# Three K parts, then three V parts: one TensorE loop over all units, and ScalarE spreads the probabilities

## The chip, the cores and the metric

The kernel runs on one core of a Trainium2 chip. The metric is the device time of one execution in microseconds (us): the median of several runs. A profiled execution also gives a span, which is the time from the first to the last recorded instruction of the core, and a trace of what each engine and each DMA queue did in it.

## The reference, cut to what matters

Two independent blocks, A and B, each do one decode step of attention with cached keys and values. Both have 2 queries (the batch), 32 heads, 8192 cached tokens and a head size of 192, all in bfloat16:

```python
q = (x @ wq)                                  # x: (2, 1, 640), wq: (640, 32*192)
scores = einsum("bhqd,bhkd->bhqk", q, k_cache) * 192 ** -0.5
p = softmax(scores, axis=-1)
o = einsum("bhqk,bhkd->bhqd", p, v_cache)     # k_cache, v_cache: (2, 32, 8192, 192)
out = o.reshape(B, 1, 32 * 192) @ wo          # wo: (6144, 640)
# the outputs of A and B side by side: (2, 1, 1280)
```

Every cached key and value is used once, for one query. The kernel therefore reads some 837 MB for a small amount of arithmetic.

## The kernel before, in words

The work is cut into 16 units. A unit is one query and 8 heads of one block (4 units for a query, 4 queries over both blocks). The K cache of a unit is laid over 128 partitions, 16 partitions a head and 512 tokens a partition, and is cut into three parts (`c` = 0, 1, 2) of 64 KiB a partition, 8 MiB a part. The V cache of a unit is cut in the same way. There are three buffers of this size (`bufs`), so of the 96 K and V parts three are on the chip at a time.

The list `loads` sets the order in which SyncE issues the transfers, all on its own queue: the three K parts of unit 0, then V part 0 of unit u-1, K part 0 of unit u, V part 1 of unit u-1, K part 1 of unit u, and so on, at the end the three V parts of unit 15 and `wo` in pieces (`pieces`). Load i goes into buffer i modulo 3, and SyncE waits before issuing it until load i-3 has been used up (`done`): for a K part until TensorE has finished its sums (`("sl", u, c)`), for a V part until TensorE has finished its products (`("pv", u, c)`). So two loads are queued behind the one that is being used.

What is done with a K part: VectorE multiplies the cached keys in place by the query (`dve_mul`, line 303), in five pieces of 32 tokens a partition (`k` = 0 to 4, the last with 10 more tokens); where a token lies across two parts its fragments go into `pad` (line 301). TensorE sums 192 products to 16 with an identity as weights (`pe_sum`, line 420, three PSUM banks in turn; `pe_rest`, line 432, for the tokens left over, whose end is `("sl", u, c)`), and VectorE reduces the 16 to the score (`dve_red`, line 311), three pieces behind its multiplications. After the third part VectorE and GpSimd find the maximum (`dve_rest`, `dve_max`, `dve_mp`, `pool_ar`, `dve_nm`, `dve_nb`), ScalarE takes the exponentials (`act_exp`, line 366), and VectorE spreads them (`dve_spread`, line 338): it writes `pb`, in which each probability stands in one of 8 columns, its head's, and the other 7 are zero. TensorE forms the row sums (`pe_l`, line 438) and multiplies `pb` with the three V parts (`pe_pv`, lines 450 and 456). VectorE and ScalarE divide and store the result (`dve_rc`, `dve_ohi`, `dve_osum`, `act_of`), and TensorE places it among the results of the other units (`pe_pl`, line 462). TensorE also makes the query of the next unit (`pe_q`), which ScalarE copies to `qt` (`act_q`).

Each engine has a list of its own (`_Stream`), filled slot by slot with `put`, in the order in which the engine works; waits are on semaphores that every step raises. In slot u TensorE, VectorE and the others do unit u's K work and unit u-1's V work. `emit` writes slot 0 and slot 16 out and the slots between as one loop.

At the start the weights `wq` for A, the input `x`, `wq` for B and the first K part are transferred. The first projection needs an identity matrix, which GpSimd and VectorE make from a triangle of ones (`tri`). At the end `pe_out` multiplies by `wo`, and two transfers store the output.

Of the kernel before, what the change touches and what calls it, by code (L numbers as in the profile page):

```python
# [12 lines left out]
class _Stream:  # L13
    virtual = set()

    def __init__(self, name, sem, reg, first=3):
# [17 lines left out]
    def resolve(self):  # L34
        waited = {}
        out = []
        for fn, waits, has_sig, tag in self.ops:
            need = {}
            for key in waits:
                if key is None or (key in self.virtual and tag[0] < self.first):  # L40
                    continue
                sem, val = self.reg[key]
                sid = id(sem)
                if val <= waited.get(sid, 0):
                    continue
                if sid not in need or need[sid][1] < val:
                    need[sid] = (sem, val)
# [8 lines left out]
    def emit(self, eng, loops=()):  # L56
        ops = self.resolve()
# [12 lines left out]
        self._emit(eng, ops[pos:])  # L70

# [48 lines left out]
def build_kernel(nc, blocks, out):  # L120
# [30 lines left out]
    PO = 128 - UH  # L151
# [4 lines left out]
    with ExitStack() as es:  # L156
# [35 lines left out]
        tri = pb[0:HP, 2304:2304 + HP + 1]  # L192
# [21 lines left out]
        S_act = _Stream("act", sem("s_act"), reg, 1)  # L214
        S_dve = _Stream("dve", sem("s_dve"), reg, 1)
        S_pool = _Stream("pool", sem("s_pool"), reg, 1)
        bsem = [sem(f"bsem{i}") for i in range(NBUF)]
# [12 lines left out]
        for u in range(1, NU):  # L230
            for c in range(NCH):
                loads += [("v", u - 1, c), ("k", u, c)]
        loads += [("v", LASTU, c) for c in range(NCH)]
        buf = {}
        for i, key in enumerate(loads):
            buf[key] = i % NBUF
            reg[key] = (bsem[i % NBUF], 16 * (i // NBUF + 1))
        for kind, u, c in loads:
            if u:
                assert buf[kind, u, c] == buf[kind, 1, c] or (kind, u) == ("v", LASTU)  # L240
# [28 lines left out]
        def ld_kv(kind, u, c):  # L269
# [3 lines left out]
            return dma(bufs[buf[kind, u, c]], src[:, c * ROW:(c + 1) * ROW], (kind, u, c))  # L273
# [21 lines left out]
        def dve_mul(u, c, k):  # L295
            b = buf["k", u, c]

            def fn(eng):
                if k == 0:
# [30 lines left out]
        def dve_spread(ranges):  # L330
            dst = pb[:].rearrange("p (g a j h) -> p g a j h", a=2, j=4, h=UH)
            src = sc[:].rearrange("p (g j a) -> p g a j", j=4, a=2)

            def fn(eng):
                for lo, hi in ranges:
                    for a in range(2):
                        shape = [128, hi - lo, 4, UH]
                        ins = eng.tensor_tensor(dst[:, lo:hi, a], src[:, lo:hi, a].unsqueeze(3).broadcast_to(shape),  # L338
                                                mask[:].unsqueeze(1).unsqueeze(1).broadcast_to(shape), ALU.mult)
                return ins  # L340
            return fn
# [119 lines left out]
        def pe_pl(u):  # L461
            return lambda eng: eng.matmul(oacc_all[:, 0:Dh], place[:, S_pe.at(UH * u, 128, UH)], o_sb[:],
# [49 lines left out]
        S_pool.add(lambda eng: eng.memset(tri, 0.0), sig=("tri0",))  # L512
        S_pool.add(lambda eng: eng.memset(ident[:], 0.0))
        for n in range(1, HP + 1):
            S_pool.add((lambda n: (lambda eng: eng.memset(tri[0:n, n:n + 1], 1.0)))(n),
                       waits=[("tri0",)] if n == 1 else [], sig=("tri",) if n == HP else None)
# [3 lines left out]
        for n in range(128 // HP):  # L520
            S_dve.add((lambda r: (lambda eng: eng.tensor_tensor(ident[r, r], tri[:, 1:HP + 1], tri[:, 0:HP], ALU.subtract)))
                      (slice(HP * n, HP * n + HP)), waits=[("tri",)], sig=("id1",) if n == 128 // HP - 1 else None)
# [28 lines left out]
        S_act.add(act_q, waits=[("q", 0)], sig=("qe", 0))  # L551
# [17 lines left out]
        for u in range(NU + 1):  # L569
# [3 lines left out]
            def red(c, k):  # L573
                put("dve", u, ("r", c, k), dve_red(u, c, k), [("s", u, c, k), ("sp", u - 1) if u else None])

            def turn_out():
# [3 lines left out]
                put("act", u, ("of", -1), act_of, [("os", v), ("rc", v), ("pl", v - 1)])  # L580

            def v_part(c):
                if c == 0:
                    put("pe", u, ("l", -1), pe_l, [("exp", v), ("sp0", v), ("os", v - 1), ("rc", v - 1)])
                put("pe", u, ("pv", c, -1), pe_pv(v, c), [("v", v, c), ("sp", v) if c else None])

            if not real:
                for c in range(NCH):
                    v_part(c)
                turn_out()  # L590
                put("pe", u, ("pl", -1), pe_pl(v), [("of", v)])
                continue
            put("dve", u, ("su", 1), dve_su(u + 1), [("q", u)])
            for c in range(NCH):
                if old:
                    v_part(c)
                for k in range(NSUB):
                    if old and c == NCH - 1 and k == 3:
                        turn_out()
                    w = [("k", u, c), ("qe", u), ("sl", u - 1, NCH - 1) if u and c == 0 else None]  # L600
                    put("dve", u, ("m", c, k), dve_mul(u, c, k), w)
                    put("pe", u, ("s", c, k), pe_sum(u, c, k), [("m", u, c, k), prev(u, c, k)])
                    if old and c == NCH - 1 and k == 3:
                        put("pe", u, ("pl", -1), pe_pl(v), [("of", v)])
                    n = NSUB * c + k - 3
                    if n >= 0:
                        red(n // NSUB, n % NSUB)
                put("pe", u, ("sl", c), pe_rest(u, c),
                    [("m", u, c, NSUB - 1), ("rl", u - 1) if u and c == 0 else None])
            c = NCH - 1  # L610
            for k in range(NSUB - 3, NSUB):
                red(c, k)
            put("dve", u, ("rl",), dve_rest, [("sl", u, c)])
            put("dve", u, ("mx",), dve_max, [("rl", u)])
            put("dve", u, ("mp",), dve_mp, [("mx", u), ("ar", u - 1) if u else None, ("negm",)])
            put("dve", u, ("nm",), dve_nm, [("ar", u)])
            put("dve", u, ("nb",), dve_nb, [("nm", u), ("exp", u - 1) if u else None])
            put("pe", u, ("q", 1), pe_q, [("su", u + 1), ("qe", u)])
            put("pool", u, ("ar",), pool_ar, [("mp", u), ("nm", u - 1) if u else None])
            put("act", u, ("qe", 1), act_q, [("q", u + 1), ("m", u, NCH - 1, NSUB - 1)])  # L620
            put("act", u, ("exp",), act_exp, [("nb", u), ("l", v) if u else None])
            g0, g1 = -(-TC // 8), TP // 8
            put("dve", u, ("sp0",), dve_spread([(0, g0), (g1 - 1, g1)]),
                [("exp", u), ("pv", v, NCH - 1) if u else None, ("mask",)])
            put("dve", u, ("sp",), dve_spread([(g0, g1 - 1)]), [])
# [107 lines left out]
```

## Time and profile before

| | |
|---|---|
| median of 3 runs | 1937.05 us (1936.92 to 1937.26) |
| the profiled execution: time, span | 1937.03 us, 1935.3 us |
| busy: TensorE, VectorE, ScalarE, GpSimd | 1531.4, 1118.9, 30.1, 8.8 us |
| moved by DMA | 836.98 MB, mean 432 GB/s over the span |
| mean granted TensorE clock | 0.927 |

A busy TensorE is not one at its peak, since matmuls are pipelined and their ends are modelled. The idle time of an engine costs nothing where another engine or a queue sets the pace. In the rows of the timeline the first number is the start and the second the duration, both in us, and the bracket at the end tells how long the engine was idle before and what ended that.

### The profile page before, as it was taken

Reading aid. Unit: us, or ns where it says so; the run is one execution under the profiler, and the core shown is the slowest. Engines: PE = TensorE matmul, PEld = TensorE weight load, DVE = VectorE, ACT = ScalarE, POOL = GpSimd, SP = SyncE. Lnnn points to the kernel's source line nnn. Section 1 sums busy time; section 2 is a strip of 40 time slices with the busy share of each in tenths; the row PEclk is TensorE's granted clock in tenths of the full one; section 3 lists DMA queues with packets and bytes.
Section 4 is the critical chain, followed back from the end, with each engine's and each line's share of the span. In section 5 each row is a group of like instructions: output and inputs, shape, how many; then the busy total and the mean of one; then the engine's idle time right before and its main releaser. Section 6 shows DMA issues by size and latency. Waiting matters only on the chain.

```text
span 1935.3 us, 18520 instructions
## 1 busy us (share of the span) xinstructions
PE 1531.4 (79%) x8255; PEld 786.8 (41%) x8256; DVE 1118.9 (58%) x835; ACT 30.1 (2%) x76; POOL 8.8 (0%) x60
## 2 busy tenths in 40 slices
PE   4678787887978778797787878778797777888779
PEld 3334343443434434353343434433343343434335
DVE  0785555846566485546846566485546846565450
ACT  0000000000000000000000000000000000000000
POOL 0000000000000000000000000000000000000000
PEclk9889898898999999999999999899998988999989
DMA  9999999999999999999999999999999999999998
GB/s 416 434 434 436 435 435 435 433 433 433 433 433 435 433 433 435 433 433 433 436 435 436 435 433 433 433 433 433 433 436 433 436 435 435 435 433 433 433 434 382
DMA packets 15149, 836.98 MB, mean 432 GB/s; under 512 B 1688, under 2 KB 1824, under 8 KB 2208
## 3 DMA queue, kind: packets, MB, share of 16 engines
q1 hardware_dynamic: 15136, 836.78, 99.8%
q8 instruction: 11, 0.18, 0.0%
q14 instruction: 2, 0.02, 0.0%
HBM read 836.77 MB, written 0.01 MB: 432 GB/s over the span
## 4 chain that ended last, share of the span: by engine, by line
DMA 38%; PE 32%; DVE 17%; issue 12%; DVEq 0%; POOL 0%; ACT 0%; SPq 0%; ACTq 0%; POOLq 0%
PE ops L450 21%; DMA big<-in_B_k_cache_dram 19%; DMA big<-in_A_k_cache_dram 16%; DVE big L303 12%; PE scps L420 9%; DVE sc L311 3%; DMA big<-in_B_wo_dram 2%; PE rest L432 1%; DMA pb<-in_B_x_dram 1%; PE scps L402 1%; DVE pb L338 1%; DVE rmax L319 0%; PE ops L456 0%; POOL mg L344 0%; DVE o_hi L350 0%
## 5 line engine op out<-in xcount | busy, mean ns | idle before, releaser
L420 PE MATMUL scps<-big,ident 128*128 128x512 bf16 x2880 | 718.7, 409 | 289.6 <-DVE sc L311 269.3
L303 DVE TENSOR_TENSOR big<-big,qt 128x6144 bf16<-128x6144 bf16 (+1 forms) x240 | 847.5, 3548 | 0.0
L450 PE MATMUL ops<-big,pb 128*40 128x384 bf16 x4080 | 709.6, 335 | 0.0
L420 PEld LDWEIGHTS scps<-big,ident 128*128 128x128 bf16 x2880 | 285.1, 104 | 707.6 <-DVE sc L311 335.9
L450 PEld LDWEIGHTS ops<-big,pb 128*40 128x40 bf16 x4080 | 413.7, 102 | 272.0 <-issue 27.7
L301 DVE TENSOR_TENSOR pad<-big,qt 128x128 bf16<-128x128 bf16 (+1 forms) x64 | 11.9, 207 | 638.5 <-DMA big<-in_B_k_cache_dram 341.5
L311 DVE TENSOR_REDUCE sc<-scps 128x32 f32<-128x512 f32 x240 | 161.0, 680 | 32.8 <-PE scps L420 32.8
L338 DVE TENSOR_TENSOR pb<-sc,mask 128x704 bf16<-128x704 f32 (+2 forms) x96 | 76.3, 864 | 14.1 <-ACT sc L366 14.1
L438 PE MATMUL ops<-rs,mask 128*8 128x1 f32 x32 | 3.1, 167 | 84.8 <-DVE pb L338 84.8
L432 PEld LDWEIGHTS rest<-big,ident 128*128 128x128 bf16 x576 | 44.8, 101 | 14.1 <-issue 4.9
L432 PE MATMUL rest<-big,ident 128*128 128x160 bf16 x576 | 49.4, 237 | 0.0
L438 PEld LDWEIGHTS ops<-rs,mask 128*8 128x8 f32 x32 | 1.6, 90 | 88.4 <-DVE pb L338 82.8
L402 PE MATMUL scps<-big,pb 128*64 128x384 bf16 x160 | 29.4, 350 | 2.8 <-DMA big<-in_B_wq_dram 2.3
L356 ACT ACTIVATE o_sb<-o_hi,rc 8x192 bf16<-8x192 f32 x16 | 7.3, 454 | 1536.9 <-DVE o_hi L353 1536.9
L347 DVE RECIPROCAL rc<-ops 8x1 f32<-8x1 f32 x16 | 2.3, 147 | 41.5 <-PE ops L450 41.5
L402 PEld LDWEIGHTS scps<-big,pb 128*64 128x64 bf16 x160 | 18.8, 119 | 13.2 <-DMA big<-in_B_wq_dram 2.7
L293 DVE TENSOR_TENSOR su<-esel,onehot 128x144 bf16<-128x144 bf16 x17 | 5.1, 300 | 30.0 <-PE outps L410 30.0
L394 PE MATMUL rest<-ident,pb 4*128 4x4 bf16 x5 | 0.4, 178 | 21.6 <-DMA pb<-in_B_x_dram 21.6
L315 DVE TENSOR_REDUCE sc<-rest 128x30 f32<-128x480 f32 x16 | 10.5, 657 | 7.5 <-PE rest L432 7.5
L344 POOL PARTITION_ALL_REDUCE mg<-mp x16 | 5.8, 366 | 1855.8 <-DVE mp L322 1855.8
L366 ACT ACTIVATE sc<-sc,nb 128x512 f32<-128x512 f32 x16 | 11.5, 721 | 32.8 <-DVE nb L328 32.8
L290 DVE CAST pb<-rest 128x5 bf16<-128x5 f32 x4 | 0.4, 171 | 19.2 <-PE rest L394 19.2
(66 smaller groups left out, 131.0 us busy)
## 6 DMA issues: line engine op xcount, KB each, us to landing
big<-in_B_wq_dram SPq DMA_DIRECT2D x1, 7680.0 KB, 37.1
big<-in_A_wo_dram SPq DMA_DIRECT2D x1, 7680.0 KB, 30.5
big<-in_A_wq_dram SPq DMA_DIRECT2D x1, 7168.0 KB, 20.1
big<-in_B_wo_dram SPq DMA_DIRECT2D x1, 4640.0 KB, 27.5
big<-in_B_wo_dram SPq DMA_DIRECT2D x1, 1760.0 KB, 31.2
big<-in_B_wo_dram SPq DMA_DIRECT2D x1, 800.0 KB, 32.6
big<-in_A_wq_dram SPq DMA_DIRECT2D x1, 512.0 KB, 3.7
big<-in_A_k_cache_dram SPq DMA_DIRECT2D x24, 38.8
```

Of the source, the lines that this page charges most:

```text
L301: eng.tensor_tensor(pad[:, t, lo:hi], src, qt[:, 0, lo:hi], ALU.mult)
L303: return eng.tensor_tensor(t, t, qt[:].broadcast_to([128, size(k), Dh]), ALU.mult)
L311: return lambda eng: eng.tensor_reduce(sc[:, lo:lo + SUB], scps[bank(u, c, k)][:], AXL.X, ALU.add)
L315: eng.tensor_reduce(dst, rest[:, 0:NCH * REST, :].rearrange("p (c t) g -> p c t g", c=NCH), AXL.X, ALU.add)
L338: ins = eng.tensor_tensor(dst[:, lo:hi, a], src[:, lo:hi, a].unsqueeze(3).broadcast_to(shape), mask[:].unsqueeze(1).unsqueeze(1).broadcast ...
L344: return eng.partition_all_reduce(mg[:], mp[:], 128, bass.bass_isa.ReduceOp.max)
L356: return eng.activation(o_sb[:], o_hi[:], ACTF.Identity, scale=rc[:])
L366: return eng.activation(sc[:], sc[:], ACTF.Exp, bias=nb[:], scale=scale, accum_out=rs[:])
L402: ins = eng.matmul(flat[blk][64 * blk:64 * blk + 64, 0:QW], xz[:, blk, c, XM - m:XM - m + 64], wq_t[blk][:, c, QW * m:QW * m + QW], start= ...
L420: ins = eng.matmul(scps[bank(u, c, k)][:], ident[:], t[:, :, j * DG:(j + 1) * DG], start=(j == 0), stop=(j == NJ - 1))
L432: ins = eng.matmul(rest[:, lo:lo + n, :], ident[:], src[:, :, j * DG:(j + 1) * DG], start=(j == 0), stop=(j == NJ - 1))
L450: ins = eng.matmul(ops[0:MP, 0:QW], pb[:, j0:j0 + MP], bufs[b][:, OFF[c] + j * QW:OFF[c] + (j + 1) * QW], start=(c == 0 and j == 0), stop= ...
```

## The change

- The order of the loads: all three K parts of unit u, then all three V parts of unit u-1. A part `c`, K or V, now always has buffer `c`, and the semaphores that count landings are one for each kind and `c`.
- The first K part of unit 0 is transferred in two pieces: the tokens of its first three fifths (`EARLY = 3`) with a semaphore of their own, then the rest. The first three multiplications wait for the first piece only.
- In slot u every engine first does unit u's K work and then unit u-1's V work. The steps `dve_nm`, `dve_nb`, `act_exp` and the spread of unit u-1 move from the end of slot u-1 into slot u: VectorE does the first two behind its first multiplication of unit u (`close`), ScalarE then the exponentials and the spread.
- The spread is done by ScalarE in 8 activations, one for each head's column (`act_spread`), and no longer by VectorE in 6 instructions.
- TensorE's loop runs over all 17 slots, with the K half under the condition `it < 16` and the V half under `it > 0` (`emit_halves`, `_half`), and its first instruction is put at a given place of a code block (`head_slot`). Before, slots 0 and 16 were written out.
- ScalarE keeps waits in its loop that an earlier wait already covers (`keep`).
- The identity is made by one `iota` on GpSimd and one comparison on VectorE.
- The five pieces of the second `wo` have 26, 12, 6, 3, 1 rows in place of 29, 11, 5, 2, 1.

```diff
+        self.keep = keep
-                if val <= waited.get(sid, 0):
+                if val <= waited.get(sid, 0) and not (self.keep and tag[0] > 0):
...
+    def emit_halves(self, eng, n, slot):
+        ops = self.resolve()
+        inner = [i for i, op in enumerate(ops) if op[3][0] in range(n + 1)]
+        lo, hi = inner[0], inner[-1] + 1
+        self._emit(eng, ops[:lo])
+        new = self._half([op for op in ops[lo:hi] if not op[3][1][1]], 0, n)
+        old = self._half([op for op in ops[lo:hi] if op[3][1][1]], 1, n + 1)
+        with eng.bass.Fori(0, n + 1, engines=[eng.engine], head_slot={eng.engine: slot}) as it:
+            with eng.If(it < n):
+                self.base = it
+                self._emit(eng, *new[:1], it, new[1])
+            with eng.If(it > 0):
+                self.base = it - 1
+                self._emit(eng, *old[:1], it - 1, old[1])
+            self.base = None
+        self._emit(eng, ops[hi:])
+
+    def _half(self, ops, lo, hi):
...
+        return out, steps     # one unit's steps, and by how much each wait grows from unit to unit
...
         for u in range(1, NU):
-            for c in range(NCH):
-                loads += [("v", u - 1, c), ("k", u, c)]
+            loads += [("k", u, c) for c in range(NCH)] + [("v", u - 1, c) for c in range(NCH)]
         loads += [("v", LASTU, c) for c in range(NCH)]
...
+            reg[key] = (bsem[key[0]][key[2]], 16 * (key[1] + 1))
+            assert buf[key] == key[2]
...
-        for blk, rows in ((0, (WR,)), (1, (29, 11, 5, 2, 1))):
+        for blk, rows in ((0, (WR,)), (1, (26, 12, 6, 3, 1))):
...
-        def dve_spread(ranges):
...
+        def act_spread(eng):
             dst = pb[:].rearrange("p (g a j h) -> p g a j h", a=2, j=4, h=UH)
             src = sc[:].rearrange("p (g j a) -> p g a j", j=4, a=2)
+            for h in range(UH):
+                ins = eng.activation(dst[:, :, :, :, h], src, ACTF.Identity, scale=mask[:, h:h + 1])
+            return ins
...
-            S_sp.add(ld_kv(*key), waits=w)
+            for part in (0, 1) if i == 0 else (None,):
+                S_sp.add(ld_kv(*key, part), waits=w)
...
-        S_pool.add(lambda eng: eng.memset(tri, 0.0), sig=("tri0",))
...
+        S_pool.add(lambda eng: eng.iota(diff, [[-1, 128]], base=0, channel_multiplier=1,
+                                        allow_small_or_imprecise_dtypes=True), sig=("diff",))
...
+        S_dve.add(lambda eng: eng.tensor_scalar(ident[:], diff, 0.0, None, ALU.is_equal), waits=[("diff",)], sig=("id1",))
...
+            def close():
+                put("dve", u, ("nm", -1), dve_nm, [("ar", v)])
+                put("dve", u, ("nb", -1), dve_nb, [("nm", v), ("exp", v - 1)])
+
+            if real:
+                put("dve", u, ("su", 1), dve_su(u + 1), [("q", u)])
+                for c in range(NCH):
+                    for k in range(NSUB):
+                        w = [("early",) if u == c == 0 and k < EARLY else ("k", u, c), ("qe", u), ("sl", u - 1, NCH - 1) if u and c == 0 else None]
+                        put("dve", u, ("m", c, k), dve_mul(u, c, k), w)
+                        put("pe", u, ("s", c, k), pe_sum(u, c, k), [("m", u, c, k), prev(u, c, k)])
+                        if old and c == k == 0:
+                            close()
+                        n = NSUB * c + k - 3
+                        if n >= 0:
+                            red(n // NSUB, n % NSUB)
+                    put("pe", u, ("sl", c), pe_rest(u, c),
+                        [("m", u, c, NSUB - 1), ("rl", u - 1) if u and c == 0 else None])
...
+                put("pe", u, ("q", 1), pe_q, [("su", u + 1), ("qe", u)])
+            else:
+                close()
+            if old:
+                put("act", u, ("exp", -1), act_exp, [("nb", v), ("l", v - 1)])
+                put("act", u, ("sp", -1), act_spread, [("exp", v), ("pv", v - 1, NCH - 1)])
+            if real:
+                put("act", u, ("qe", 1), act_q, [("q", u + 1), ("m", u, NCH - 1, NSUB - 1)])
+            if old:
+                put("pe", u, ("l", -1), pe_l, [("exp", v), ("os", v - 1), ("rc", v - 1)])
+                for c in range(NCH):
+                    put("pe", u, ("pv", c, -1), pe_pv(v, c), [("v", v, c), ("sp", v) if c == 0 else None])
                 put("dve", u, ("rc", -1), dve_rc, [("pv", v, NCH - 1), ("of", v - 1)])
                 put("dve", u, ("oh", -1), dve_ohi, [("of", v - 1)])
                 put("dve", u, ("os", -1), dve_osum, [("oh", v)])
                 put("act", u, ("of", -1), act_of, [("os", v), ("rc", v), ("pl", v - 1)])
+                put("pe", u, ("pl", -1), pe_pl(v), [("of", v)])
...
-                S_pe.emit(eng, [(1, NU, 1)])
+                S_pe.emit_halves(eng, NU, 232)
```

More of the change, by code (lines that the diff above doesn't have):

```diff
@@ L593, in build_kernel @@
[L593 to L618, printed above, removed]
@@ L643, in build_kernel @@
                 for n, fn, waits, _ in slots[e][u]:
[L644 to L646 removed]
+                    if e == "pe":
+                        S.add(fn, waits=waits, sig=full(n, u), tag=(u, (n, n[0] in OLD, tuple(waits))))
+                        continue
+                    head = u == 0 and n == slots[e][0][0][0]
+                    gone = [("qa", "qe")] if e == "act" and u == NU and n[0] == "of" else after.get(None, ()) if head else ()
+                    S.add(fn, waits=waits, sig=full(n, u), tag=(u, n), pre=gone, post=after.get(n, ()) if u == 0 else ())
+        for n in (("l",), ("pv", NCH - 1), ("pl",)):
+            key = lambda v: (n[0], v) + n[1:]
+            reg[key(-1)] = (S_pe.sem, 2 * reg[key(0)][1] - reg[key(1)][1])
         S_dve.add(dve_oall(0), waits=[("pl", LASTU), ("q", NU)], sig=("oa", 0))
```

103 lines of the change are left out of this document (51 added, 52 removed).

## The prediction, made before the changed kernel was run

> **What bounds the kernel now.** I read the page from its slices down, then the landings of single loads on VectorE's timeline, then SyncE's issues. The page first:
>
> ```profile
> PE 1531.4 (79%) x8255; PEld 786.8 (41%) x8256; DVE 1118.9 (58%) x835; ACT 30.1 (2%) x76; POOL 8.8 (0%) x60
> ...
> DMA  9999999999999999999999999999999999999998
> GB/s 416 434 434 436 435 435 435 433 433 433 433 433 435 433 433 435 433 433 433 436 435 436 435 433 433 433 433 433 433 436 433 436 435 435 435 433 433 433 434 382
> q1 hardware_dynamic: 15136, 836.78, 99.8%
> q8 instruction: 11, 0.18, 0.0%
> DMA 38%; PE 32%; DVE 17%; issue 12%; DVEq 0%; POOL 0%; ACT 0%; SPq 0%; ACTq 0%; POOLq 0%
> ```
>
> The DMA engines are full in every slice. The chain (last row) is misleading: it runs through TensorE and VectorE because each transfer was issued after them, but a transfer issued into a queue that still holds another waits for that one. Whether the queue ever ran dry shows in the landings, where VectorE waits for a K part:
>
> ```profile
> 79.56 0.29 DVE L301 TENSOR_TENSOR pad<-big,qt 128x64 bf16<-128x64 bf16 x2 [0.53 <-DMA big<-in_A_k_cache_dram]
> ...
> 100.11 0.21 DVE L301 TENSOR_TENSOR pad<-big,qt 128x128 bf16<-128x128 bf16 x1
> ...
> 103.51 0.68 DVE L311 TENSOR_REDUCE sc<-scps 128x32 f32<-128x512 f32 x1
> 104.11 3.35 DVE L303 TENSOR_TENSOR big<-big,qt 128x6144 bf16<-128x6144 bf16 x1
> ...
> 119.98 1.88 DVE L311 TENSOR_REDUCE sc<-scps 128x32 f32<-128x512 f32 x3
> 125.20 0.69 DVE L311 TENSOR_REDUCE sc<-scps 128x32 f32<-128x512 f32 x1 [3.35 <-PE scps L420]
> ...
> 127.84 0.23 DVE L322 TENSOR_SCALAR mp<-negm,rmax 128x8 f32<-128x8 f32 x1
> ...
> 128.77 0.16 DVE L328 TENSOR_REDUCE nb<-nm 128x1 f32<-128x8 f32 x1
> 129.81 4.77 DVE L338 TENSOR_TENSOR pb<-sc,mask 128x704 bf16<-128x704 f32 x6 [0.88 <-ACT sc L366]
> 134.50 0.30 DVE L293 TENSOR_TENSOR su<-esel,onehot 128x144 bf16<-128x144 bf16 x1
> 137.47 0.22 DVE L301 TENSOR_TENSOR pad<-big,qt 128x128 bf16<-128x128 bf16 x1 [2.68 <-DMA big<-in_A_k_cache_dram]
> ...
> 214.90 0.23 DVE L301 TENSOR_TENSOR pad<-big,qt 128x128 bf16<-128x128 bf16 x1 [18.19 <-DMA big<-in_A_k_cache_dram]
> ```
> ```profile
> 60.27 0.22 DVE L301 TENSOR_TENSOR pad<-big,qt 128x128 bf16<-128x128 bf16 x1 [4.78 <-DMA big<-in_A_k_cache_dram]
> ```
> ```profile
> 1837.58 0.23 DVE L301 TENSOR_TENSOR pad<-big,qt 128x128 bf16<-128x128 bf16 x1 [18.03 <-DMA big<-in_B_k_cache_dram]
> ```
>
> Counting the K and V parts from 0 in order of issue, 79.56 is the landing of load 1, 137.47 of load 4, 214.90 of load 8, 1837.58 of load 92. Load 1 to load 92: 1758.02 us / 91 = 19.32 us each. Load 4 by this would land at 137.52 and load 8 at 214.80, as they do. So the queue never ran dry, and it gives the same rate beside a busy VectorE and an idle one:
>
> ```profile
> 79.50:98.90 19.40, 15.74 (x71) 6.75 (x69) 19.34 (x11) 0.00 (x0) 0.00 (x0) 0.91 1.01 434
> ...
> 156.90:176.20 19.30, 18.64 (x116) 10.86 (x114) 0.12 (x2) 0.00 (x0) 0.00 (x0) 1.00 1.01 435
> ```
>
> (After the stretch's length: busy TensorE, its weight loads, VectorE, ScalarE, GpSimd; then clock, DMA share, GB/s.) The kernel is bound by the bytes at a constant rate. An edit inside the units changes the time only if it lets the queue run dry.
>
> The room for that: load i may be issued only when load i-3 is used up, and must be issued before load i-1 has landed, by 60.24 + 19.32 (i-1), less the delay of a transfer that finds an empty queue. The first transfer of all bounds the delay:
>
> ```profile
> big<-in_A_wq_dram SPq DMA_DIRECT2D x1, 512.0 KB, 3.7
> ```
>
> 512 KB at 434 GB/s are 1.2 us, so 2.5 us are delay (an estimate). The Trainium skill, page "DMA: Bandwidth & Descriptors", section "Anatomy of one DMA — SWDGE (gpsimd) path", fits about 2.0 us fixed for a transfer on GpSimd's path; by that, against 2.5 in the trace, the stall below would be 0.5 us shorter.
>
> **The order of the loads, at the start.** This is where the change can cost time. Six K parts now come in a row (units 0 and 1), before any V part, and VectorE takes longer over a K part than its transfer does: load 1's work runs from 79.56 to 100.11, 20.55 us against 19.32. The early first piece doesn't help: VectorE gets through load 0 sooner, but it already waits 0.53 us for load 1 at 79.56, and that lands no earlier. So up to `dve_mp` of unit 0, at 127.84 + 0.23 = 128.07, VectorE's timeline stays that of before. From there:
>
> - `dve_su` 0.30; the first K part of unit 1 from 128.4: 20.55, less three reductions of 0.60 (103.51 to 104.11) that belong to the unit before, plus `nm` and `nb` at about 0.2 each (0.16 in `nb`'s row): 19.1, to 147.5. Second part 20.55: to 168.05. Third: to 188.6.
> - From the last reduction that frees a bank to the freed buffer, the rows of TensorE and SyncE:
>
> ```profile
> 120.72 4.45 PE L420 MATMUL scps<-big,ident 128*128 128x512 bf16 x12 [2.10 <-DVE sc L311]
> ...
> 126.32 0.33 SPq L254 DMA_DIRECT2D big<-in_A_v_cache_dram  x1
> ```
> ```profile
> 1743.08 2.76 PE L420 MATMUL scps<-big,ident 128*128 128x512 bf16 x12 [1.92 <-DVE sc L311]
> ...
> 1747.00 0.33 SPq L254 DMA_DIRECT2D big<-in_B_v_cache_dram  x1
> ```
>
> That is 5.6 us where the twelve sums take 4.45, and 3.9 where they take 2.76. After VectorE's longest piece at the start the slow form is there, so I take 5.6, for a third part; a first or second one has no `pad` to sum, 0.5 less.
>
> - Load 6 (V part 0 of unit 0) issues at 147.5 + 0.1 + 5.1 = 152.7; needed by 156.8 - 2.5 = 154.3: no stall. Load 7: 168.05 + 5.2 = 173.3, needed by 173.7: just in time. Load 8: 188.6 + 5.7 = 194.3, needed by 195.5 - 2.5 = 193.0: **1.3 us of stall**. With the fast form it issues at 192.6: none.
> - Load 9 waits for the first V product of unit 0. TensorE comes to it after the sums and the query, at about 195; rows of the products:
>
> ```profile
> 1869.22 15.45 PE L450 MATMUL ops<-big,pb 128*40 128x384 bf16 x85
> ...
> 1884.75 13.99 PE L450 MATMUL ops<-big,pb 128*40 128x384 bf16 x85
> ```
>
> 195 + 15.5 = 210.5, needed by 214.8 + 1.3 - 2.5 = 213.6. No stall, and V parts are worked off in 14.0 against 19.32, so the lag goes.
>
> **The order, later units.** With T the landing of a unit's first part, the three K buffers are free at T + 24, 45 and 66, needed at T + 36, 55 and 75 (38.6, 58.0, 77.3 less 2.5). The V products end at T + 82, 96 and 111, needed by T + 94, 113 and 133; VectorE's division then waits for the third and holds up the next multiplication, but T + 112 lies ahead of T + 116. So about 9 us spare in each unit. Before it was 11 (126.32 against 137.5) at its tightest in the rows above; no gain in either.
>
> **The spread on ScalarE.** VectorE is relieved of 4.77 us a unit, which gains nothing: it stood idle for 18 us ahead of a landing. ScalarE's cost, with the nearest rows:
>
> ```profile
> L366 ACT ACTIVATE sc<-sc,nb 128x512 f32<-128x512 f32 x16 | 11.5, 721 | 32.8 <-DVE nb L328 32.8
> L363 ACT ACTIVATE qc<-scps 64x384 bf16<-64x384 f32 x2 | 1.0, 484 | 51.3 <-PE scps L402 51.3
> L338 DVE TENSOR_TENSOR pb<-sc,mask 128x1312 bf16<-128x1312 f32 x32 | 47.3, 1518 | 0.0
> ```
>
> Eight activations of 512 elements at 0.48 (384 elements to bfloat16) to 0.72 (512 to float32) are 3.9 to 5.8 us; I take 0.72. Its output goes to every eighth element, as the spread on VectorE does in 1.52 us for 1312 elements: 1.52 is the upper end, 12.1 us. VectorE's first reduction of unit u waits for it, since it overwrites the scores. That stands behind four multiplications of some 3.3 us. In unit 1: the first multiplication ends at 131.8 and `nb` at 132.2, exponentials to 133.2, spread to 139.0, reduction due at 142.0. Hidden, with 3.0 us to spare; without that cover every us goes into load 8's stall, once. Queued behind the spread on ScalarE are `act_q` and `act_of`, due 40 us later.
>
> **Edits that cost nothing.** The identity: the first projection's input lands late,
>
> ```profile
> 21.59 0.35 PE L394 MATMUL rest<-ident,pb 4*128 4x4 bf16 x5 [21.59 <-DMA pb<-in_B_x_dram]
> ```
>
> so an `iota` of up to 18 us is covered, and with it the memsets queued behind it on GpSimd. One more DMA issue: 0.33 us of a SyncE that issues one load in 19 us. ScalarE's kept waits: it is idle 98% of the span. The end: the last `wo` row sets it, not the engines,
>
> ```profile
> 1932.12 0.50 PEld L484 LDWEIGHTS scps<-big,oT 128*2 128x2 bf16 x10 [0.57 <-DMA big<-in_B_wo_dram]
> ...
> 1932.88 0.09 PEld L484 LDWEIGHTS scps<-big,oT 128*2 128x2 bf16 x4 [0.26 <-DMA big<-in_B_wo_dram]
> 1933.26 0.08 PEld L484 LDWEIGHTS scps<-big,oT 128*2 128x2 bf16 x2 [0.29 <-DMA big<-in_B_wo_dram]
> 1933.60 0.43 ACT L386 ACTIVATE pb<-scps 2x320 bf16<-2x320 f32 x1 [9.12 <-PE scps L484]
> ```
>
> and other cuts of the same bytes land at the same 1933.3 (0.38 us a row: two rows from 1932.12 to 1932.88, one to 1933.26). I allow 0.2 us either way.
>
> **TensorE's loop and conditions.** Between units 0 and 1 it jumps over the V half at about 126.8 and has nothing to do until 131.8: 5 us of cover. Later back edges fall into the wait for a landing (T + 113 to T + 119). The trace has no row for a branch; I take 0, and 3.7 us, the landing of the smallest load above, as its upper end, covered at this jump too. The Trainium skill, page "Runtime: NRT & Kernel Launch", section "Instruction fetch mechanics", says that a taken branch whose target isn't in a window of two pages must fetch it first. The trace speaks against it for a loop of this size: 11 instruction packets in all, though the loop of before closes 14 times. By the rule the sum would still be the same, for the cover named.
>
> **Sum.** 1937.03 us (the profiled execution; 0.02 below the median of the runs, 1.7 around its span) + 1.3 for load 8 + 0 = **1938.3 us**, +0.07%. A measurement of this kernel can tell about 0.2%, 3.9 us, from no change.
>
> **Rivals.**
> - *No stall at all*: the sums before load 8 go fast (2.76), or the delay is shorter than 2.5. 1937.0. The row at 1743.08 speaks for it, that at 120.72 against.
> - *Slower, by the spread*: ScalarE needs more than 1.1 us for each activation, and the first reduction of unit 1 is late. At 1.52 the spread ends at 145.4, 3.4 late, and load 8's stall grows to 4.7: 1941.7. It decides above 0.2% from 1.43 us each. Later units absorb it. The bfloat16 outputs of ScalarE speak against it.
> - *Slower, by the loop*: instruction fetches delay the first sums of unit 1 or the first V product of unit 0 by more than the cover of 5.0 and 3.1 us. No row prices a fetch behind a full queue; 10 us ahead of unit 1 would give 1.3 + 5.0 of stall, 1943.3, and 7.6 us decide. The packet count speaks against it.
> - *Faster*: the bytes move faster when runs of three parts are contiguous. Loads 0 and 1, two K parts in a row, are 79.56 - 60.27 = 19.29 apart, 0.03 less than the mean: 96 times this is 2.9 us, 1934.1. VectorE's start isn't an exact landing, and three V parts or more bytes a run aren't in the trace; for over 0.2% the gain must be 0.04 a load.
>
> **How the numbers follow.** Forecast (a stall up to 3 us) 0.58, no stall 0.28, spread 0.06, loop 0.05, faster 0.03. The first two are within 0.2%, 0.86 and a little of the spread's case: same 0.87, slower 0.10, faster 0.03. The range goes from 1936.0 (no stall, 0.2 at the end, something of the rate) to 1941.7 (the spread's upper end).
>
> **What the new profile would show.** VectorE busy near 1043 us (76.3 less at line 338, by 16 times 4.77), ScalarE's up by 16 times 3.9 to 5.8, to 92 to 123; the DMA slices as before. SyncE's issue of load 8 near 194, and the landing of unit 2's first K part near 234.1 + 1.3; landings 19.32 apart from there; no wait of VectorE for DMA in unit 1. The prediction is wrong if slices lose DMA share in the middle, if a reduction waits for ScalarE, or if the landings come at another pace.

## The result, and the profile after

The changed kernel takes 1997.27 us (median of 6 runs, 1979.2 to 2004.6) against 1937.04 us (6 runs, 1936.92 to 1937.26): ratio 1.0298, 95% interval 1.0252 to 1.0344. It is slower, by 60 us, where 1.3 us were forecast. The profiled execution of it took 2004.6 us, with a span of 2003.1 us.

From its page: busy times, DMA slices, the load queue, and the two groups that matter. At the end of a group stand busy us, mean ns of one, and idle time before it with what ended it.

```profile
PE 1562.5 (78%) x8255; PEld 788.2 (39%) x8256; DVE 1041.6 (52%) x736; ACT 326.6 (16%) x204; POOL 7.9 (0%) x27
...
DMA  9998999999999999999999999999999999999997
GB/s 415 437 435 365 423 419 419 419 419 423 415 428 431 412 425 419 419 419 419 440 398 440 419 419 437 400 440 398 440 419 419 419 419 440 411 424 421 417 420 315
...
q1 hardware_dynamic: 15280, 836.78, 97.7%
...
L382 ACT ACTIVATE pb<-sc,mask 128x512 bf16<-128x512 f32 x128 | 296.7, 2755 | 1.7
L359 DVE TENSOR_REDUCE sc<-scps 128x32 f32<-128x512 f32 x240 | 161.0, 682 | 199.2 <-ACT pb L382 147.3
```

The same bytes move, but many slices show 419 GB/s or less where it was 433 to 435. (The DMA row still shows 9 in these slices, but a 9 only means 90% or more.) ScalarE is busy for 326.6 us where the forecast had 92 to 123; one activation of the spread takes 2755 ns. VectorE's reductions waited 147.3 us for it. VectorE's 1041.6 us are as forecast (1043). In the list of waits (total, times, longest):

```profile
DVE sc L359 <- ACT pb L382: 147.3, 15, 9.8
...
PE ops L492 <- ACT pb L382: 17.8, 1, 17.8
```

The wait comes 15 times, at 9.8 us: in every unit from 1 to 15, not in the first alone. That the load queue runs dry shows in the time from issue to landing of A's V parts, first in the changed kernel, then in the kernel before:

```profile
big<-in_A_v_cache_dram SPq DMA_DIRECT2D x24, 21.8
```
```profile
big<-in_A_v_cache_dram SPq DMA_DIRECT2D x24, 33.6
```

21.8 us is one transfer of 19.3 and the 2.5 of delay: since this is the median, half of these loads or more found the queue as good as empty. Before, they stood 12 us behind another transfer. All three signs by which the prediction called itself wrong are there: the reductions wait for ScalarE, the slices in the middle lose speed, and the pace differs. One unit in the middle, from the timeline of the changed kernel:

```profile
962.70 3.35 DVE L351 TENSOR_TENSOR big<-big,qt 128x6144 bf16<-128x6144 bf16 x1
...
967.37 18.56 ACT L382 ACTIVATE pb<-sc,mask 128x512 bf16<-128x512 f32 x8
...
985.96 0.69 DVE L359 TENSOR_REDUCE sc<-scps 128x32 f32<-128x512 f32 x1 [9.83 <-ACT pb L382]
...
1032.58 4.45 PE L462 MATMUL scps<-big,ident 128*128 128x512 bf16 x12 [2.10 <-DVE sc L359]
...
1038.80 13.99 PE L492 MATMUL ops<-big,pb 128*40 128x384 bf16 x85
...
1052.87 13.99 PE L492 MATMUL ops<-big,pb 128*40 128x384 bf16 x85
...
1066.94 13.83 PE L492 MATMUL ops<-big,pb 128*40 128x384 bf16 x84
1080.80 0.16 DVE L389 RECIPROCAL rc<-ops 8x1 f32<-8x1 f32 x1 [40.87 <-PE ops L492]
...
1082.14 3.35 DVE L351 TENSOR_TENSOR big<-big,qt 128x6144 bf16<-128x6144 bf16 x1
```

Read it as one chain. VectorE starts on the unit's keys at 962.70, stands still for 9.83 us, and is followed by TensorE's last sums at 1032.58. Then come the three V products back to back (none of them waits for a landing), 1038.4 to 1080.8, then VectorE's division, then the next unit at 1082.14. K half and V half lie one after the other, so the unit takes 1082.14 - 962.70 = 119.44 us, and no wait for a landing is in it. Without the stall it would be 109.6; six landings take 115.9. A unit can therefore hide 6.3 us of stall. It has 9.8, and pays 3.5, fifteen times. SyncE's issues (the second number spans the three issues of the group) show the period:

```profile
160.91 41.62 SPq L300 DMA_DIRECT2D big<-in_A_v_cache_dram  x3
...
398.24 43.15 SPq L300 DMA_DIRECT2D big<-in_A_v_cache_dram  x3
...
517.69 43.12 SPq L300 DMA_DIRECT2D big<-in_A_v_cache_dram  x3
...
1831.58 85.51 SPq L300 DMA_DIRECT2D big<-in_B_v_cache_dram  x6
```

From 398.24 to 517.69 is one unit, 119.45 us; from 160.91 to 1831.58 are 14, 119.33 us each.

### The profile page after: what moved, and what is told of

Same layout as the page of the kernel before. It is cut to its first block, busy times and chain, and to the rows that moved or that the text cites. A ratio compares the mean times of both kernels' runs of the same rounds, so it can differ in the third digit from the quotient of the medians.

```text
span 2003.1 us, 18709 instructions
## 1 busy us (share of the span) xinstructions
PE 1562.5 (78%) x8255; PEld 788.2 (39%) x8256; DVE 1041.6 (52%) x736; ACT 326.6 (16%) x204; POOL 7.9 (0%) x27
## 5 line engine op out<-in xcount | busy, mean ns | idle before, releaser
L462 PE MATMUL scps<-big,ident 128*128 128x512 bf16 x2880 | 785.7, 434 | 367.8 <-DVE sc L359 315.8
L492 PE MATMUL ops<-big,pb 128*40 128x384 bf16 x4080 | 675.8, 327 | 17.8 <-ACT pb L382 17.8
L462 PEld LDWEIGHTS scps<-big,ident 128*128 128x128 bf16 x2880 | 298.3, 109 | 837.6 <-DVE sc L359 397.5
L492 PEld LDWEIGHTS ops<-big,pb 128*40 128x40 bf16 x4080 | 404.4, 100 | 270.3 <-ACT pb L382 17.9
L382 ACT ACTIVATE pb<-sc,mask 128x512 bf16<-128x512 f32 x128 | 296.7, 2755 | 1.7
L359 DVE TENSOR_REDUCE sc<-scps 128x32 f32<-128x512 f32 x240 | 161.0, 682 | 199.2 <-ACT pb L382 147.3
L401 ACT ACTIVATE qt<-outps 128x192 bf16<-128x192 f32 x17 | 5.6, 331 | 857.7 <-PE outps L452 857.7
L444 PEld LDWEIGHTS scps<-big,pb 128*64 128x64 bf16 x160 | 18.6, 117 | 11.7 <-DMA big<-in_B_wq_dram 1.4
```

The source lines that it names most:

```text
L359: return lambda eng: eng.tensor_reduce(sc[:, lo:lo + SUB], scps[bank(u, c, k)][:], AXL.X, ALU.add)
L382: ins = eng.activation(dst[:, :, :, :, h], src, ACTF.Identity, scale=mask[:, h:h + 1])
L444: ins = eng.matmul(flat[blk][64 * blk:64 * blk + 64, 0:QW], xz[:, blk, c, XM - m:XM - m + 64], wq_t[blk][:, c, QW * m:QW * m + QW], start= ...
L462: ins = eng.matmul(scps[bank(u, c, k)][:], ident[:], t[:, :, j * DG:(j + 1) * DG], start=(j == 0), stop=(j == NJ - 1))
L492: ins = eng.matmul(ops[0:MP, 0:QW], pb[:, j0:j0 + MP], bufs[b][:, OFF[c] + j * QW:OFF[c] + (j + 1) * QW], start=(c == 0 and j == 0), stop= ...
```

## The experiments

**The changed kernel again.** No edit.

> The changed kernel once more, for a second trace: its six times lay between 1979 and 2005, those of before within 0.4 us. Theory H: a unit's time is now VectorE and TensorE in turn, so it takes in how fast TensorE's sums go; in another execution the last twelve sums of a K part take 2.8 in place of 4.45 us, or a unit's first V product goes slower, and the unit's period differs by 1 to 2 us from 119.4, constant or nearly so within a run. Rival: the activations' own length varies from run to run.

2004.78 us in one run, with the same wait and a period of 119.4 us throughout. The period is that of the first profile, so this run doesn't show the difference of 1 to 2 us that was expected; the run with the source in a row, below, does.

**The output of the spread in a row.** Each activation writes its 512 values next to each other; the instructions are the same in kind and number. The products then take their weights from the wrong places, so only the time means something.

```diff
-            dst = pb[:].rearrange("p (g a j h) -> p g a j h", a=2, j=4, h=UH)
+            dst = pb[:].rearrange("p (h g a j) -> p h g a j", h=UH, a=2, j=4)
...
-                ins = eng.activation(dst[:, :, :, :, h], src, ACTF.Identity, scale=mask[:, h:h + 1])
+                ins = eng.activation(dst[:, h], src, ACTF.Identity, scale=mask[:, h:h + 1])
```

> The changed kernel, but each of the eight activations writes its 512 values side by side (a block for each head) and not to every eighth element; the products then use wrong columns. Same count, same type, the source as before. If the 16-byte steps of the output make an activation 2.3 us long: some 0.6 to 0.75 each, spread 5 to 6 us, the kernel 1938 to 1942. If the source's steps do it: 2.3 each and 1980 to 2005, as changed.

1937.07 us in one run, beside 1937.43 (median of 7) for the kernel before. From its timeline, its groups and SyncE's issues:

```profile
131.24 5.39 ACT L382 ACTIVATE pb<-sc,mask 128x512 bf16<-128x512 f32 x8
```
```profile
L382 ACT ACTIVATE pb<-sc,mask 128x512 bf16<-128x512 f32 x128 | 86.3, 757 | 1.7
```
```profile
149.15 43.31 SPq L300 DMA_DIRECT2D big<-in_A_v_cache_dram  x3
...
1765.41 89.91 SPq L300 DMA_DIRECT2D big<-in_B_v_cache_dram  x6
```

The spread is 5.39 us, near the forecast's 5.8, and the whole loss is gone. The rest of the change (order, loop, conditions, first piece, identity, `wo` pieces) costs nothing in sum here; no run takes these edits one by one. The issues also give the account of the profiled 2003.1 us against this kernel's span of 1935.6, 67.5 us. Load 6 comes 11.8 later (160.91 against 149.15). The 14 units to the V parts of unit 14 take 1670.7 instead of 1616.3, 54.4 more. (That is 3.9 a unit and not 3.5, because the cheap kernel's first interval between these issues is only 111.2, 149.15 to 260.36: it is behind at the start and catches up.) From there to the end it is 171.5 instead of 170.2, 1.3 more.

**The source of the spread in a row.** The activations read the scores in the order of their addresses and write as in the changed kernel.

```diff
-            src = sc[:].rearrange("p (g j a) -> p g a j", j=4, a=2)
+            src = sc[:].rearrange("p (g a j) -> p g a j", j=4, a=2)
```

> The changed kernel, but each activation reads the 512 scores in the order in which they lie, and not every second one; its output still goes to every eighth element, so the columns hold wrong tokens. If the output's steps are the cause: 2.3 us each and 1980 to 2005, as changed. If the source's: some 0.7 each and 1938 to 1942.

1994.01 us in one run. From its timeline:

```profile
982.48 0.69 DVE L359 TENSOR_REDUCE sc<-scps 128x32 f32<-128x512 f32 x1 [9.82 <-ACT pb L382]
...
1029.10 2.77 PE L462 MATMUL scps<-big,ident 128*128 128x512 bf16 x12 [2.10 <-DVE sc L359]
```

The stall is the same 9.82 us, so the order of reading is not the price; the spacing of the writing is.

**Output steps of 1, 2 and 4.** Six activations for each unit, whose outputs stand 1, 1, 2, 2, 4 and 4 elements apart, on lines of their own. Two heads are left out, and the products take weights from the wrong places.

```diff
...
+            eng.activation(dst(1, 0, 0), src, ACTF.Identity, scale=mask[:, 0:1])
+            eng.activation(dst(1, 3584, 0), src, ACTF.Identity, scale=mask[:, 1:2])
+            eng.activation(dst(2, 512, 0), src, ACTF.Identity, scale=mask[:, 2:3])
+            eng.activation(dst(2, 512, 1), src, ACTF.Identity, scale=mask[:, 3:4])
+            eng.activation(dst(4, 1536, 0), src, ACTF.Identity, scale=mask[:, 4:5])
+            return eng.activation(dst(4, 1536, 1), src, ACTF.Identity, scale=mask[:, 5:6])
```

> The cost of an activation by the step of its output, measured by itself: in the changed kernel the spread is six activations of 512 elements, two each with a step of 1, 2 and 4 elements of 2 bytes, into parts of the probabilities' tile that don't overlap (zeroed once; the result is no attention). Step 8 took 2.32 us from one to the next, a row of values 0.67. If the time goes with the step: about 0.7, 0.9, 1.4. If any step breaks it: 0.7, 2.3, 2.3. The kernel: spread under 11 us, so hardly a reduction waits, 1937 to 1942.

1938.29 us in one run, beside 1937.19 (median of 13). One unit in its timeline:

```profile
1052.97 0.77 ACT L383 ACTIVATE pb<-sc,mask 128x512 bf16<-128x512 f32 x1
1053.65 0.76 ACT L384 ACTIVATE pb<-sc,mask 128x512 bf16<-128x512 f32 x1
1054.31 0.86 ACT L385 ACTIVATE pb<-sc,mask 128x512 bf16<-128x512 f32 x1
1055.04 0.85 ACT L386 ACTIVATE pb<-sc,mask 128x512 bf16<-128x512 f32 x1
1055.75 1.42 ACT L387 ACTIVATE pb<-sc,mask 128x512 bf16<-128x512 f32 x1
1056.91 1.41 ACT L388 ACTIVATE pb<-sc,mask 128x512 bf16<-128x512 f32 x1
```

From start to start: 0.7 us at a step of 1, 0.7 at 2, 1.2 at 4. The changed kernel's step of 8 has 18.56 / 8 = 2.3. So a step of 2 costs next to nothing, one of 4 costs 0.5 us, and from 4 to 8 the time doubles; no run has a larger step.

**One head fewer, and two.** The activation of head 7, or of heads 6 and 7, is left out of the spread (the edit shown is that for seven; for six it says `range(6)`).

```diff
-            for h in range(UH):
+            for h in range(7):
...
+        S_pool.add(lambda eng: eng.memset(pb[:], 0.0), waits=[("q", 0)], sig=("pbz",))
```

> The spread leaves out the last of its eight activations (head 7 of each unit gets no probabilities; its columns are zeroed once at the start by GpSimd). Theory A: spread 16.2 us, the reduction 7.5 late, a unit 117.1, so 1.2 us lost in each of 15 units, some 8 at the start and 3 at the end: 1955 to 1970. Rival E (the prediction's reckoning: 9 us spare in every unit, paid once at the start): 1945.

> Two of the eight activations left out (heads 6 and 7, their columns zeroed once). Theory A: spread 13.9 us, the reduction 5.2 late, a unit 114.8, under the 115.9 of the transfers: only the start pays, 1.3 + 5.2, 1941 to 1946. Rival F (the cost goes in proportion to ScalarE's time, whatever the pace): 1997 less a quarter of 60, 1982.

Seven: 1953.23 us (1951.42 to 1954.02), ratio 1.0083 (1.0067 to 1.0100). Six: 1941.63 us (1940.89 to 1943.54), ratio 1.0024 (1.0014 to 1.0033). The reductions' wait, seven first, then six:

```profile
DVE sc L359 <- ACT pb L382: 113.3, 15, 7.6
```
```profile
DVE sc L359 <- ACT pb L382: 79.3, 15, 5.3
```

Each activation taken away shortens the stall by its own 2.3 us: 9.8, 7.6, 5.3. The time doesn't follow in proportion: over the kernel before it is 60, 16 and 4 us. With 109.6 us of other work the sum for a unit is 119.4, 117.2 and 114.9, the first two above the 115.9 of six landings, the third below. SyncE's issues with seven heads:

```profile
156.86 41.62 SPq L300 DMA_DIRECT2D big<-in_A_v_cache_dram  x3
...
1781.99 84.24 SPq L300 DMA_DIRECT2D big<-in_B_v_cache_dram  x6
```

Only some of the 14 units between them take 116.9 us, the others 115.5 to 115.8, and the mean is 116.1. So with seven heads the units themselves lose only some 0.2 us each, less than I expected. Most of the 16 us lies at the start and the end: load 8 goes out at 156.86 + 41.62 - 0.33 = 198.2, 5.1 us after the 193.0 at which the queue needed it, and ahead of the last V products TensorE waits 15.5 us for the spread, which nothing hides there. With six heads the units are hidden again, and load 8 goes out 3.2 us late (196.2). How the rest divides in these two runs isn't worked out.

**The scores held apart.** The exponentials go to a PSUM bank of their own, from which ScalarE spreads them; the reductions wait for the exponentials, no longer for the spread, which stays as slow as it was.

```diff
+        pr = ps("pr", [128, TP], F32)
...
-            return eng.activation(sc[:], sc[:], ACTF.Exp, bias=nb[:], scale=scale, accum_out=rs[:])
+            return eng.activation(pr[:], sc[:], ACTF.Exp, bias=nb[:], scale=scale, accum_out=rs[:])
...
-                put("dve", u, ("r", c, k), dve_red(u, c, k), [("s", u, c, k), ("sp", v) if old else None])
+                put("dve", u, ("r", c, k), dve_red(u, c, k), [("s", u, c, k), ("exp", v) if old else None])
```

> The changed kernel, but the exponentials go to a tile of their own (a free PSUM bank), so VectorE's reductions wait for the exponentials and no longer for the spread, which stays on ScalarE in eight activations. Theory A: no reduction waits for ScalarE any more, a unit takes 119.4 - 9.8 = 109.6 of work, DMA sets the pace; the start costs about 1.3 and the end up to 4 us, where the last spread stands between the last V parts: 1938 to 1943. Rival D (the slow activations cost by themselves, by TensorE's wait for the spread or by traffic with VectorE): stays above 1980.

1941.93 us (1939.16 to 1943.64, 10 runs), ratio 1.0024 (1.0014 to 1.0034). 55 of the 60 us are gone with the one wait, though ScalarE is as busy as before. What is left is the end, where the last spread lies between the last K part and the V products:

```profile
1857.31 18.35 ACT L383 ACTIVATE pb<-pr,mask 128x512 bf16<-128x512 f32 x8
...
1875.71 0.51 PE L493 MATMUL ops<-big,pb 128*40 128x384 bf16 x1 [17.70 <-ACT pb L383]
...
1906.05 2.23 SPq L301 DMA_DIRECT2D big<-in_B_wo_dram  x5
```

The second `wo` so starts at 1906.05 against 1892.76 in the kernel with the output in a row.

**The spread back on VectorE.** The new order, with the spread in two VectorE instructions behind the third multiplication.

```diff
...
+                        if old and c == 0 and k == 2:
+                            put("dve", u, ("sp", -1), dve_spread, [("exp", v), ("pv", v - 1, NCH - 1)])
...
-                put("act", u, ("sp", -1), act_spread, [("exp", v), ("pv", v - 1, NCH - 1)])
```

> The changed kernel with the spread back on VectorE (two instructions, some 4.8 us, behind the third multiplication of the unit); order of loads, TensorE's loop and conditions, and all else as changed. Theory A (eight activations of 2.3 us hold VectorE's first reduction 9.8 us in every unit, and K half and V half then take 119.4 us in turn on VectorE and TensorE, over the 115.9 us of six transfers): the unit takes 119.4 - 9.8 + 4.8 = 114.4, under 115.9, so DMA sets the pace again; lost is only the start, about 1.3 + 4.8 us at load 8: 1940 to 1945. Rival B (the new order itself, three K parts and then three V parts, costs the time): stays above 1980. Rival C (TensorE's conditional loop costs it, by code fetches at each jump): stays above 1980.

1940.95 us (1939.91 to 1942.16, 10 runs), ratio 1.0019 (1.0010 to 1.0029). Timeline and issues:

```profile
136.83 4.49 DVE L383 TENSOR_TENSOR pb<-sc,mask 128x2048 bf16<-128x2048 f32 x2
...
1900.05 0.51 PE L494 MATMUL ops<-big,pb 128*40 128x384 bf16 x1 [5.06 <-DMA big<-in_B_v_cache_dram]
```
```profile
155.42 41.63 SPq L300 DMA_DIRECT2D big<-in_A_v_cache_dram  x3
```

Here 4.49 us of VectorE's own time stand in the K half. Load 8, the third issue of the group, goes out at 155.42 + 41.63 - 0.33 = 196.7, 3.7 us after the 193.0 at which the queue needed it, and 3.7 us is what the kernel loses. The last V part lands 4.4 us after the pace (60.24 + 95 times 19.32 = 1895.64); with the output in a row it lands 1.5 us after it (1897.17), so the two 3.7 agree more closely than the landings do. This is the stall paid once, as the prediction described it: 4.5 us a unit are under 6.3, so the later units hide it.

**The spread alone, in the old order.** The kernel before, its spread moved to ScalarE and nothing else.

```diff
...
-            put("dve", u, ("sp0",), dve_spread([(0, g0), (g1 - 1, g1)]),
-                [("exp", u), ("pv", v, NCH - 1) if u else None, ("mask",)])
-            put("dve", u, ("sp",), dve_spread([(g0, g1 - 1)]), [])
+            put("act", u, ("sp",), act_spread, [("exp", u), ("pv", v, NCH - 1) if u else None, ("mask",)])
```

> The kernel before, with one part of the change alone: the spread by ScalarE in eight activations. All else, the old order of loads and TensorE's loop too, as before. Theory A (the 18.6 us spread is the cause, the order is not): in the old order the first V product waits for the whole spread, 16.7 us later than before (1769.1 against 1752.4 in the unit at 1747), its buffer comes free 8 us too late, and K part to K part the loop of waits is some 124 us instead of 115.9: 2030 to 2060. Rival G (the spread on ScalarE costs only together with the new order): 1937 to 1945.

2087.93 us (2083.9 to 2091.09), ratio 1.0772 (1.0754 to 1.0790): further up than I expected. Its timeline, a wait, and two of SyncE's issues, a unit apart:

```profile
1004.57 18.49 ACT L334 ACTIVATE pb<-sc,mask 128x512 bf16<-128x512 f32 x8
...
1023.11 0.51 PE L444 MATMUL ops<-big,pb 128*40 128x384 bf16 x1 [18.33 <-ACT pb L334]
```
```profile
PE ops L444 <- ACT pb L334: 293.3, 16, 18.4
```
```profile
1001.08 0.33 SPq L254 DMA_DIRECT2D big<-in_A_v_cache_dram  x1
...
1126.18 0.33 SPq L254 DMA_DIRECT2D big<-in_B_v_cache_dram  x1
```

In the old order the first V product follows the spread at once, and TensorE waits 18.4 us in each unit; the unit takes 125.1 us. So the spread is the loss, and the new order doesn't cause it but hides part of it (a unit of 119.4 us instead of 125.1).

**Runs of eight.** The complete kernel, with the 8 values of a head that follow each other in `pb` written in a row; TensorE then reads its weights with a step of 8.

```diff
-            dst = pb[:].rearrange("p (g a j h) -> p g a j h", a=2, j=4, h=UH)
+            dst = pb[:].rearrange("p (g a j h t) -> p g a j t h", a=2, j=4, h=UH, t=8)
...
-                    ins = eng.matmul(ops[0:MP, 0:QW], pb[:, j0:j0 + MP],
+                    ins = eng.matmul(ops[0:MP, 0:QW], pb[:, j0:j0 + 8 * MP - 7:8],
...
```

> The changed kernel with another layout of the probabilities: for each head eight tokens stand side by side (64 runs of 8 elements a head, where it was 512 single elements, 16 bytes apart), and TensorE reads its 40 weight columns with a step of 8 elements. Nothing is left out. If what slows the activations is that every element is written by itself: 0.7 to 0.9 us each, spread 6 to 7, no reduction waits, 1937 to 1940. If weights with a step load slower than the 163 ns that a product takes, the V half grows (over 20 us a part) and the unit passes 115.9 us: above 1950.

1937.22 us (1936.11 to 1938.85, 10 runs) against 1937.19, ratio 1.0001 (0.9991 to 1.0011). Its groups:

```profile
L382 ACT ACTIVATE pb<-sc,mask 128x512 bf16<-128x512 f32 x128 | 85.3, 751 | 1.7
...
L492 PEld LDWEIGHTS ops<-big,pb 128*40 128x40 bf16 x4080 | 610.0, 151 | 124.9 <-DMA big<-in_A_v_cache_dram 27.0
```

An activation is back at 751 ns. A weight load costs 151 ns instead of 100, which stays beside the products, whose waits are for V parts again. This is the time of the kernel before and not less: none of the versions gets below the rate of the DMA.

## Why the prediction was wrong

**The step that failed first is the price of the spread.** It took 0.72 us for each activation from rows whose outputs stand in a row, and as upper end VectorE's row of 1.52, 12.1 us a unit, because VectorE's spread was said to write to every eighth element too. It doesn't: `dve_spread` of the kernel before writes `dst[:, lo:hi, a]`, where the 8 columns of 4 tokens follow each other, so VectorE wrote runs of 32 values. No row of the trace had ScalarE's pattern on any engine. Measured: 18.56. So ScalarE's price wasn't between the two rows, and the range built on them couldn't hold it. The spread takes as long (18.44 us) at the end, where VectorE and TensorE stand still, so it isn't contention with these two:

```profile
1918.98 18.44 ACT L382 ACTIVATE pb<-sc,mask 128x512 bf16<-128x512 f32 x8
...
1937.47 0.51 PE L492 MATMUL ops<-big,pb 128*40 128x384 bf16 x1 [17.79 <-ACT pb L382]
```

The Trainium skill, page "ScalarE: Activation LUTs", section "What ACT_TABLE_LOAD costs", gives one element per cycle and lane, and its figures make about 0.61 us from one such activation to the next (an estimate: 0.186 + 0.093 + 512 times 0.00083, less 0.093 of overlap). The runs agree roughly for outputs in a row, 0.67, and contradict that one rate for a step of 8, 2.32.

**The second is "later units absorb it".** The rival "Slower, by the spread" had the mechanism right: the first reduction waits for the spread, behind four multiplications. With 18.6 us put into its own arithmetic the reduction comes at 133.2 + 18.6 = 151.8, 9.8 late, which is what the trace shows. But it charged this once, to load 8; that would have given 1937.0 + 1.3 + 9.8 = 1948.1, 49 us too little. The "9 us spare in each unit" was the margin of the loads. It left out that a stall of VectorE in the K half moves the V products, the division and the next unit along with it. The prediction's own sentence on the division (T + 112 against T + 116) had the true limit, some 4 us. The trace gives 6.3. The runs with six and seven heads fit: a stall of 5.3 costs the units nothing, and one of 7.6 only a little.

**What held.** The DMA rate is the floor, at 19.32 us a landing. VectorE's shorter work gains nothing. The order, the loop, the conditions, the identity and the `wo` pieces cost nothing in sum, as the kernel with the output in a row shows. The early first piece gains nothing: VectorE waits for load 1 instead,

```profile
DVE pad L349 <- DMA big<-in_A_k_cache_dram: 5.4, 1, 5.4
```

in one wait of 5.4 us. Load 8's stall seems to come and go with the slow sums on the way to it. In the kernel with steps of 1, 2 and 4,

```profile
151.11 43.31 SPq L300 DMA_DIRECT2D big<-in_A_v_cache_dram  x3
```

SyncE issued it at 151.11 + 43.31 - 0.33 = 194.1 (forecast 194.3, needed by 193.0), and that run was 1.1 us over the kernel before, one run only. With the output in a row it was issued at 149.15 + 43.31 - 0.33 = 192.1, in time, and with the runs of eight at 192.1 too (150.83 + 41.62 - 0.33). So with a cheap spread the runs came to 1937.07, 1937.22 and 1938.29 us: between the rival without a stall (1937.0) and the forecast (1938.3), and too close together to tell which.

**What was too small but didn't matter.** TensorE's jump over the V half after unit 0:

```profile
133.09 18.56 ACT L382 ACTIVATE pb<-sc,mask 128x512 bf16<-128x512 f32 x8
133.88 10.24 PE L462 MATMUL scps<-big,ident 128*128 128x512 bf16 x36 [7.48 <-issue]
```

7.48 us idle, where the upper end was 3.7 and the cover 5.0. The first sums came 2.2 us after their input (131.68), and the reductions weren't waiting for them yet. The Trainium skill, page "Runtime: NRT & Kernel Launch", section "Instruction fetch mechanics", says that a taken branch whose target lies outside a window of two pages must fetch that page first. The trace has an idle time at this jump that would fit, released by nothing that it shows, but it doesn't show that a fetch ended it; and it has no such idle time at the later turns of the loop.

**The spread of the runs.** From 1979.2 to 2004.6 is 25.4 us, while the versions bound by DMA vary by 5 us or less. Once a unit is bound by its engines, TensorE's last twelve sums count: 4.45 us in the row at 1032.58, 2.77 in that at 1029.10 (the kernel with its source in a row), both after 2.10 us of idleness. 1.7 us in 15 units are 25 us. The kernel with its source in a row shows both in one run: seven units in a row, from SyncE's issue at 638.53 to that at 1462.71, take 117.7 us each, and the units before and after them 119.4. The two speeds are two granted clocks. From 1032.58 to 1034.00 and from there to 1035.50, in the slow sums, the profile's windows have a granted clock of 0.60 and 0.50; from 1029.10 to 1031.87, in the fast sums of the other run, 1.00. The six runs of the changed kernel stand in the same order by their mean clock, from 0.932 for 1979.2 us down to 0.901 for 2004.6. Why the clock is granted in one case and not in the other, after the same idleness, is open.

## What to carry to other kernels

Price an instruction by a row with the same engine and the same access pattern, and read the pattern in the code: VectorE's spread and ScalarE's fill the same tile, but one in runs of 32 values and the other value by value. Where the trace has no such row, there is no upper end to take from it. When K and V work of a unit become one chain, add up the chain and compare it with the period of the transfers: a stall below the difference is paid once or not at all, one above it is paid in every unit. If an output must be scattered, let another step scatter it: runs of eight values brought the activation from 2.3 to 0.7 us, and the step moved to a weight load that had room.

## What the runs showed of the hardware

ScalarE's activation of 512 values to bfloat16 took 0.7 us with outputs 1 or 2 elements apart, 1.2 at 4, 2.3 at 8 (16 bytes), and 0.67 with runs of eight in a row; the order of the source made no difference (18.55 us for eight, against 18.56). VectorE's spread of the same values, in runs of 32, took 4.49 us. A weight load of 40 columns took 151 ns with a step of 16 bytes and 100 ns without. Twelve sums took 2.77 us at a granted clock of 1.00 and 4.45 us where it was 0.50 to 0.60 for most of them. A jump of TensorE over half a unit's instructions left it idle for 7.5 us while the load queue was full, and cost no time here.
